# Rounding weights on ScalarE, loading them through Pool's queue, and new rules for VectorE's pieces

## The chip, the core and the metric

One core of one Trainium2 chip. The metric is the device time of one execution in microseconds (us); for the kernel before it is 1285.2 us, the median of three runs (1283.07 to 1286.11). Engines: TensorE (PE; PEld is its weight load), VectorE (DVE), ScalarE (ACT), GpSimd (POOL, "Pool"), SyncE (SP). SP computes nothing here and issues most of the DMAs, in order. Every engine works through its own instructions in order; between engines there are semaphores.

## The reference

`x` is 2048 x 512. The output is `g * a + (1 - g) * b`, where `g` is a sigmoid per row, `a` is attention and `b` a two-layer network on the same `x`:

```
g = sigmoid((x * gate_w).sum(-1))
q = (x @ wq) as 32 heads of 16;  k = x @ wk;  v = x @ wv        # one k and v for all heads
a = softmax(q k^T / 4) v, heads side by side, @ wo              # 32 x 2048 x 2048 exponentials
h = relu(x @ w1 + b1)^2                                          # 512 -> 1792
b = h @ w2 + b2                                                  # 1792 -> 512
```

All in float32.

## The kernel before

**Precision.** A float32 matrix `w` is split in two tiles: `r`, rounded to the multiplier's format, and `l = w - r`. A product is three matmuls, `r r + r l + l r` (`pairs`, L174). `split` (L170) does both steps on VectorE: L171 rounds, L172 subtracts.

**Attention.** Work is cut in 32 iterations `it`: chunk `c` of 512 query rows (4) by group of 4 heads (8). Each has 32 units `u`, half a chunk of queries against 128 keys. `scores` (L598) runs two matmuls into a bank pair `s` (two such pairs exist), and ScalarE takes the exponential of 128 x 1024 (L609). `context` (L612) multiplies the exponentials into `acc` (L620). `finish` (L637) copies `acc` with ScalarE (L647, for each iteration but the last two), and `unpack` (L220) separates outputs `oc` from denominators `lc` with two DMAs on SP. `divide` (L628) divides on VectorE, in `pieces` of 128 columns, four for a pair of iterations; then Pool's queue stores the result `oTs` (L662). `ask` (L700) loads it back and splits it, and `projection` (L731) multiplies by `wo`.

**The network.** `hidden` (L508) computes one tile of `h` (128 of the 1792 columns) for one chunk from one w1 tile; `summed` (L531) adds a group of four or three tiles into the chunk's result with their w2 tiles. Over the four chunks, 56 w1 tiles and 56 w2 tiles of 128 x 512 are loaded and split (n counts them). `w_load` (L414) allocates one float32 tile per half, `w1f` or `w2f`, and loads it on SP's queue; `w_split` (L421) rounds and subtracts on VectorE and asks for the next load, so a tile's load begins when its predecessor has been split. `room` says how many split tiles may exist.

**The order.** The program is written out by a planner at build time. `stream` (L181) turns the network, the q products and the projections into slots: one slot is two matmuls of 64 rows, half 0 now and half 1 five slots later (`LAG`). A unit has 12 slots in general, 9 where `summed` has three tiles. When a half is complete, its evacuation is issued to VectorE at once. There are three PSUM banks for units, of which each takes two. `phase` (L795) puts together some units of attention and some slots: a full phase has 4 score units and 8 slots, a light phase 2 units and 2 or 3 slots. `plan` (L817) chooses by the slots that are left: the first 174 phases are full, the others light. At the head of each phase stand a piece of division from `side` and then `turn_of_chores` (L493): first what is in `soon`; then `w_split` for tiles whose load is due by the planner's own clock (`w_ready`: more than `LANDS` = 4 us since issue; a phase counts 4.9 or 2.1 us); then one of the `chores` (loading and splitting `x` again for chunks 2 and 3, `wo`, and attention results). A chore that loads holds up the others for 6 us of that clock. If the generator reaches a tile that isn't split, `have` (L489) splits it on the spot.

If `projection` must wait for `ask`, it yields None and the phase's remaining slots are empty.

The loads of q for the next iteration (L406), `unpack`, the weight loads, and the loads of `x`, `wo` and `oT` share SP's queue. Pool's queue has stores, and the scaling of `b2` (L541, four per chunk).

At most two things of this kind were given out at the head of a full phase, one in a light one (`count`, L497).

Of the kernel before, what the change touches and what calls it, by code (L numbers as in the profile page):

```python
# [23 lines left out]
NG = 8  # L24
# [9 lines left out]
WARM = 12  # L34
LANDS = 4.0
# [5 lines left out]
Q_ROWS = (0, 0, DH), (DH, 0, DH), (RS + 1, DH + 1, KS), (RS, DH, DH + 1)  # L41

# [100 lines left out]
def mix_kernel(ctx: ExitStack, tc: tile.TileContext, xT, wkv, wq, wo, w12, b1, b2, cst, out):  # L143
# [16 lines left out]
    ok = keep.tile([128, NC * KT * 4], F32, name="ok")  # L160
# [85 lines left out]
    with fast, tc.tile_pool(name="at", bufs=1) as at, \  # L246
# [163 lines left out]
        wf, since, ws = ({}, {}), ({}, {}), ({}, {})  # L410
# [3 lines left out]
        def w_load(half):  # L414
            n = len(wf[half])
            if n < NC * NF:
                wf[half][n] = at.tile([128, 512], F32, name=f"w{half + 1}f")
                since[half][n] = clock
                nc.sync.dma_start(wf[half][n], w12[n % NF, :, half * 512:half * 512 + 512])

        def w_split(half):  # L421
            n = len(ws[half])
            assert n < room[half]
            ws[half][n] = [at.tile([128, 512], F32R, name=f"w{half + 1}{x}", bufs=3 + half) for x in "rl"]
            split(*ws[half][n], wf[half][n])
            w_load(half)

        def w_ready(half):
            n = len(ws[half])
            return n in since[half] and n < min(room[half], NC * NF) and clock - since[half][n] > LANDS  # L430

# [50 lines left out]
        held = 0.0  # L482
        chores, soon = [], [lambda: wq_split(2, nc.vector), lambda: wq_split(3, nc.vector), lambda: w_load(0), lambda: w_load(1)]
# [9 lines left out]
        def turn_of_chores(slots):  # L493
# [3 lines left out]
            count = 2 if slots > 3 and (not side or w_ready(0) and w_ready(1)) else 1  # L497
            if soon:
                return soon.pop(0)()
            for half in (1, 0):  # L500
                if count and w_ready(half):
                    w_split(half)
                    count -= 1
            if count and chores and clock > held:
                if chores.pop(0)():
                    held = clock + LANDS + 2

        def hidden(c, f, hs):  # L508
# [5 lines left out]
            (wr, wl), (r, l) = ws[0][n], x[c]  # L514

# [40 lines left out]
        def x_again(c):  # L556

            r, l = [xp.tile(sh, F32R, name=f"x{n}again{c}", tag=f"x{n}{c - 2}") for n in "rl"]
            f = []

            def load():
                f.append(keep.tile(sh, F32, name="xf", tag="r2"))
                nc.sync.dma_start(f[0], xT[:, c * CH:(c + 1) * CH].rearrange("(k p) s -> p k s", p=128))
                return True

            def part(k):
                split(r[:, k], l[:, k], f[0][:, k])
# [3 lines left out]
            chores.append(load)  # L571
            for k in range(KT):
                later(part, k)
# [50 lines left out]
        ol = {}  # L624
# [284 lines left out]
```

## Time and profile before

| | |
|---|---|
| median of the runs | 1285.2 us (1283.07 to 1286.11) |
| the profiled execution's own time | 1283.75 us |
| its span, first to last instruction | 1281.7 us |
| mean granted TensorE clock | 0.986 |
| busy: TensorE / ScalarE / VectorE / Pool | 1250.9 / 1014.0 / 630.2 / 59.9 us |
| DMA moved | 85.58 MB, 67 GB/s mean |

How to read the lines of the profile below. A group: line, engine, operation, written tile <- read tiles, shape, x count, then | busy us, mean ns of one | idle time just before them, and what ended it. A wait: who waited, <- for whom: us in total, times, longest. A row of a timeline: start, duration, engine, line, operation, x count, and in brackets idle time before it and what ended that. SPq means SP's instruction queue. A window: start:end, length, then the busy time (and count) of each engine in the order PE, PEld, DVE, ACT, POOL, then granted clock, DMA share and GB/s; a window of one source line shows only the engine that has it. A row of the chain of waits: start, duration, what it was. DMA rows: tile, engine, count, KB each, median us from issue to landing.

### The profile page before, as it was taken

Reading aid. Unit: us, or ns where it says so; the run is one execution under the profiler, and the core shown is the slowest. Engines: PE = TensorE matmul, PEld = TensorE weight load, DVE = VectorE, ACT = ScalarE, POOL = GpSimd, SP = SyncE. Lnnn points to the kernel's source line nnn. Section 1 sums busy time; section 2 is a strip of 40 time slices with the busy share of each in tenths; the row PEclk is TensorE's granted clock in tenths of the full one; section 3 lists DMA queues with packets and bytes.
Section 4 is the critical chain, followed back from the end, with each engine's and each line's share of the span. In section 5 each row is a group of like instructions: output and inputs, shape, how many; then the busy total and the mean of one; then the engine's idle time right before and its main releaser. Section 6 shows DMA issues by size and latency. Waiting matters only on the chain.

```text
span 1281.7 us, 23432 instructions
## 1 busy us (share of the span) xinstructions
PE 1250.9 (98%) x9702; PEld 622.2 (49%) x9702; DVE 630.2 (49%) x1173; ACT 1014.0 (79%) x1083; POOL 59.9 (5%) x68
## 2 busy tenths in 40 slices
PE   7999999999999999999999999999999999999997
PEld 5555545554555555445555555555433333333333
DVE  6454664727567544466745576256262344231412
ACT  5678778786777777767877777877899999999984
POOL 1001120000002000000010000002000000000000
PEclk9799999998999999999999999999999999999998
DMA  6243321202122121112212122122010120010100
GB/s 203 78 127 86 97 96 38 87 24 73 63 104 82 47 88 47 44 57 92 87 54 71 46 91 71 55 77 73 29 61 29 38 87 30 30 54 30 54 34 35
DMA packets 46563, 85.58 MB, mean 67 GB/s; under 512 B 11828, under 2 KB 13492, under 8 KB 45940
## 3 DMA queue, kind: packets, MB, share of 16 engines
q1 hardware_dynamic: 39348, 68.28, 16.4%
q0 software_dynamic: 6816, 15.23, 3.5%
q8 instruction: 78, 1.28, 0.4%
q10 hardware_dynamic: 288, 0.52, 0.1%
q14 instruction: 33, 0.27, 0.1%
HBM read 55.15 MB, written 20.97 MB: 59 GB/s over the span
## 4 chain that ended last, share of the span: by engine, by line
PE 89%; DVE 5%; DMA 2%; SPq 1%; issue 1%; ACT 0%; DVEq 0%; ACTq 0%
PE acc L620 35%; PE mm L207 29%; PE s L605 23%; DMA w2f<-in_w 1%; PE mm L179 1%; SPq L406 1%; DVE n L634 1%; DVE w2l L172 1%; DMA wof<-in_wo 1%; DMA xf<-in_xT 0%; DVE w2r L171 0%; DVE big L521 0%; DVE w1l L172 0%; DVE big L522 0%; DVE hr L172 0%
## 5 line engine op out<-in xcount | busy, mean ns | idle before, releaser
L609 ACT ACTIVATE e<-s 128x1024 f32<-128x1024 f32 x1024 | 981.0, 1023 | 226.4 <-PE s L605 222.7
L620 PE MATMUL acc<-e,v_ext 128*32 128x512 f32 x4096 | 510.8, 602 | 0.0
L605 PE MATMUL s<-qa,k_aug 49*128 49x512 f32 x2048 | 460.9, 438 | 5.0 <-DMA qa<-qs 4.8
L605 PEld LDWEIGHTS s<-qa,k_aug 49*128 49x128 f32 x2048 | 198.6, 186 | 344.2 <-ACT e L609 313.9
L544 DVE SCALAR_TENSOR_TENSOR res<-mm,omg,res 128x512 f32<-128x512 f32 x128 | 96.0, 750 | 269.0 <-PE mm L207 269.0
L207 PE MATMUL mm<-w2r,hr 64*128 64x512 f32 x896 | 214.3, 396 | 4.8 <-DVE big L517 3.9
L620 PEld LDWEIGHTS acc<-e,v_ext 128*32 128x32 f32 x4096 | 98.7, 109 | 207.3 <-issue 203.6
L207 PE MATMUL mm<-w2l,hr 64*128 64x512 f32 x448 | 160.1, 395 | 0.0
L207 PEld LDWEIGHTS mm<-w2r,hr 64*128 64x128 f32 x896 | 130.3, 188 | 22.2 <-DVE big L517 4.8
L207 PEld LDWEIGHTS mm<-w2l,hr 64*128 64x128 f32 x448 | 84.2, 188 | 7.3
L207 PE MATMUL mm<-xr,w1r 64*128 64x512 f32 x224 | 77.5, 394 | 4.4 <-DVE big L521 2.4
L207 PE MATMUL mm<-xragain,w1l 64*128 64x512 f32 x224 | 79.5, 391 | 0.0
L207 PE MATMUL mm<-xragain,w1r 64*128 64x512 f32 x224 | 78.5, 393 | 0.9 <-DVE big L517 0.8
L207 PE MATMUL mm<-xlagain,w1r 64*128 64x512 f32 x224 | 78.7, 391 | 0.0
L207 PE MATMUL mm<-xr,w1l 64*128 64x512 f32 x224 | 78.5, 391 | 0.0
L207 PE MATMUL mm<-xl,w1r 64*128 64x512 f32 x224 | 78.0, 392 | 0.0
L521 DVE TENSOR_TENSOR big<-big,mm 128x512 f32<-128x512 f32 x56 | 38.4, 686 | 79.8 <-PE mm L207 79.7
L517 DVE TENSOR_SCALAR big<-mm,b1t 128x512 f32<-128x512 f32 x56 | 42.0, 750 | 49.9 <-PE mm L207 47.9
L634 DVE RECIPROCAL n<-n 128x128 f32<-128x128 f32 x60 | 57.2, 953 | 2.1
L171 DVE CAST w2r<-w2f 128x512 fp32r<-128x512 f32 x56 | 23.6, 421 | 51.4 <-DMA w2f<-in_w 51.3
L207 PEld LDWEIGHTS mm<-xr,w1r 64*128 64x128 f32 x224 | 41.3, 186 | 10.7 <-DVE big L521 3.4
L207 PE MATMUL mm<-xr,wqr 64*128 64x512 f32 x120 | 44.4, 424 | 1.9 <-DVE qf L369 1.9
(137 smaller groups left out, 1128.6 us busy)
## 6 DMA issues: line engine op xcount, KB each, us to landing
w1f<-in_w SPq DMA_DIRECT2D x56, 256.0 KB
w2f<-in_w SPq DMA_DIRECT2D x56, 256.0 KB
qa<-qs SPq DMA_DIRECT2D x192, 64.0 KB
xf<-in_xT SPq DMA_DIRECT2D x8, 512.0 KB
qs<-qr SPq DMA_DIRECT2D x16, 256.0 KB
ress<-res POOLq DMA_DIRECT2D x4, 1024.0 KB, 4.2
qs<-ql POOLq DMA_DIRECT2D x15, 256.0 KB, 8.6
oc<-accs SPq DMA_DIRECT2D x30, 128.0 KB
```

Of the source, the lines that this page charges most:

```text
L171: nc.vector.tensor_copy(r, src)
L172: nc.vector.tensor_tensor(l, src, r.bitcast(F32), OP.subtract)
L179: nc.tensor.matmul(ps, a, b, start=first and i == 0, stop=last and i == len(terms) - 1)
L207: nc.tensor.matmul(banks[half], a[rows], b[rows], start=i == 0, stop=i == len(terms) - 1)
L406: nc.sync.dma_start(q[64 * r + row:64 * r + row + b - a].bitcast(F32), qs[it, r, a:b])
L517: nc.vector.tensor_scalar(h[0], p, b1t[:, f:f + 1], None, op0=OP.add)
L521: nc.vector.tensor_tensor(h[0], h[0], p, OP.add)
L544: nc.vector.scalar_tensor_tensor(part, p, omg[:, s:s + 1], part, op0=OP.mult, op1=OP.add)
L605: nc.tensor.matmul(s[:, r].rearrange("p (a n) -> p a n", a=2), k_aug[rows, kt * 128:(kt + 1) * 128], qa[it][rows, :, cols], start=True, st ...
L609: nc.scalar.activation(es[u // 2][:, :, cols], s.rearrange("p r (a n) -> p (r a) n", a=2), AF.Exp, scale=SCALE)
L620: nc.tensor.matmul(acc[h * 32:(h + 1) * 32, cols], v_ext[:, i % NK], es[i][:, h % 2 * 2 + h // 2, cols], start=(i % NK == 0), stop=(i % NK ...
L634: nc.vector.reciprocal(n, n)
```

## The change

- Each half (w1, w2) now has two float32 places and loads two tiles ahead: `w_load` of tile n+2 goes to the place of tile n, right behind n's subtraction. The second place of each half lies in a new tile `stage`, which takes the buffer (tag `r2`) that held whole loads of `x`, `wo` and `oT`. These now come in halves of two tiles, through the other half of `stage`.
- The weight loads are issued on Pool's queue (`nc.gpsimd`) and no longer on SP's.
- The split is parted: `w_round` rounds, `w_rest` subtracts on VectorE and issues the load. In full phases the rounding is an ACTIVATE Copy on ScalarE, issued at the end of the phase, behind its last exponential, for each half that is ready; the subtraction follows at the head of the next phase. In light phases, and where `have` forces a tile, both stay on VectorE.
- `turn_of_chores` counts a budget of VectorE time per phase (2.7, or 2.4 in light phases; 1.2 less with a division at hand; 0.7 per subtraction, 1.1 per split). A chore needs more than 1.0 left. Which half goes first depends on how many w1 tiles are ahead.
- A division comes in six parts of 86 columns (the last of 82), and the generator idles one turn before the first in full phases, two in light ones. The store is issued with the last part, no longer one turn behind it.

```diff
+BUDGET = 2.7
+PARTS = [slice(a, min(a + 86, CH)) for a in range(0, CH, 86)]
...
         def w_load(half):
             n = len(wf[half])
             if n < NC * NF:
-                wf[half][n] = at.tile([128, 512], F32, name=f"w{half + 1}f")
+                if n < 2:
+                    if n and not stage:
+                        stage.append(keep.tile(sh, F32, name="stage", tag="r2"))
+                    place = stage[0][:, 2 + half] if n else at.tile([128, 512], F32, name=f"w{half + 1}f")
+                else:
+                    place = wf[half][n - 2]
+                wf[half][n] = place
                 since[half][n] = clock
-                nc.sync.dma_start(wf[half][n], w12[n % NF, :, half * 512:half * 512 + 512])
+                nc.gpsimd.dma_start(wf[half][n], w12[n % NF, :, half * 512:half * 512 + 512])
+
+        def w_round(half, copy):
+            n = len(rounded[half])
+            assert n < room[half]
+            rounded[half][n] = [at.tile([128, 512], F32R, name=f"w{half + 1}{x}", bufs=3 + half) for x in "rl"]
+            copy(rounded[half][n][0], wf[half][n])
+
+        def w_rest(half):
+            n = len(ws[half])
+            r, l = ws[half][n] = rounded[half][n]
+            nc.vector.tensor_tensor(l, wf[half][n], r.bitcast(F32), OP.subtract)
+            w_load(half)
+
+        def scalar_copy(out, src):
+            nc.scalar.activation(out, src, AF.Copy)
 
         def w_split(half):
...
+            if len(rounded[half]) == len(ws[half]):
+                w_round(half, nc.vector.tensor_copy)
+            w_rest(half)
...
-            count = 2 if slots > 3 and (not side or w_ready(0) and w_ready(1)) else 1
             if soon:
                 return soon.pop(0)()
-            for half in (1, 0):
-                if count and w_ready(half):
+            spare = (BUDGET if slots > 3 else BUDGET - 0.3) - (1.2 if side else 0.0)
+            for half in halves():
+                if len(rounded[half]) > len(ws[half]):
+                    w_rest(half)
+                    spare -= 0.7
+                elif slots < 4 and spare > 1.0 and w_ready(half):
                     w_split(half)
-                    count -= 1
-            if count and chores and clock > held:
+                    spare -= 1.1
+            if spare > 1.0 and chores and clock > held:
                 if chores.pop(0)():
                     held = clock + LANDS + 2
+
+        def halves():
+            return (0, 1) if len(ws[0]) < begun[0] + 2 else (1, 0)
...
         def x_again(c):
...
+            def load(a):
+                nc.sync.dma_start(stage[0][:, :2], xT[a * 256:a * 256 + 256, c * CH:(c + 1) * CH]
+                                  .rearrange("(k p) s -> p k s", p=128))
                 return True
...
         def pieces(it, c, t, o, l):
-            for _ in range(2):
+            for _ in range(1 if many[0] else 2):
                 yield
-            for q in range(4):
-                i = 4 * (4 * c + t) + q
-                divide(t, o, l, slice(q * 128, q * 128 + 128), ok[:, i:i + 1])
-                yield
+            for q, cols in enumerate(PARTS):
+                i = len(PARTS) * (4 * c + t) + q
+                divide(t, o, l, cols, ok[:, i:i + 1])
+                if q < len(PARTS) - 1:
+                    yield
             nc.gpsimd.dma_start(oTs[it - 1:it + 1].rearrange("u d n -> (u d) n"), o)
...
             for u in us:
                 scores(u)
+            for half in halves():
+                if slots > 3 and not soon and w_ready(half):
+                    w_round(half, scalar_copy)
```

More of the change, by code (lines that the diff above doesn't have):

```diff
@@ L159, in mix_kernel @@
     b1t = keep.tile([128, NF], F32, name="b1t")
-    ok = keep.tile([128, NC * KT * 4], F32, name="ok")
+    ok = keep.tile([128, NC * KT * len(PARTS)], F32, name="ok")
     bad = keep.tile([1, 1], I32, name="bad")
@@ L407, in q_load @@
             qa[it] = q
-        wf, since, ws = ({}, {}), ({}, {}), ({}, {})
+        wf, since, rounded, ws = ({}, {}), ({}, {}), ({}, {}), ({}, {})
+        stage = []
         room = [3, 4]
@@ L514, in hidden @@
             (wr, wl), (r, l) = ws[0][n], x[c]
+            begun[0] += 1
             def first(p):
@@ L622, in context @@
                                      skip_group_check=True, tile_position=(0, h * 32))
-        ol = {}
+        ol, many = {}, [True]
         complete = set()
@@ L628, in divide @@
         def divide(t, o, l, cols, okc):
-            n = at.tile([128, 128], F32, name="n")
+            n = at.tile([128, 86], F32, name="n")[:, :cols.stop - cols.start]
             nc.vector.tensor_scalar(n, l[:, cols], L_MIN, L_MAX, op0=OP.max, op1=OP.min)
@@ L706, in ask, with load @@
             tiles = []
-            def load():
-                tiles.extend((keep.tile(sh, F32, name="oT", tag="r2"), keep.tile(sh, F32R, name="orr", tag="r3"),
-                              xp.tile(sh, F32R, name="orl", tag="xl3")))
-                nc.sync.dma_start(tiles[0][:, :n], oTs[c * NG:c * NG + 2 * n].rearrange("(t u) d n -> (u d) t n", u=2))
+            def load(a):
+                if a == 0:
+                    tiles.extend((keep.tile(sh, F32R, name="orr", tag="r3"), xp.tile(sh, F32R, name="orl", tag="xl3")))
+                m = min(2, n - 2 * a)
+                i = c * NG + 4 * a
+                nc.sync.dma_start(stage[0][:, :m], oTs[i:i + 2 * m].rearrange("(t u) d n -> (u d) t n", u=2))
                 return True
             def part(t):
-                oT, orr, orl = tiles
-                split(orr[:, t], orl[:, t], oT[:, t])
+                orr, orl = tiles
+                split(orr[:, t], orl[:, t], stage[0][:, t % 2])
                 if t == n - 1:
                     osp[c] = orr, orl
-            chores.append(load)
             for t in range(n):
+                if t % 2 == 0:
+                    chores.append(lambda t=t: load(t // 2))
                 later(part, t)
@@ L798, in phase @@
             us = list(us)
+            many[0] = slots > 3
             if ripe:
```

41 lines of the change are left out of this document (17 added, 24 removed).

## The prediction

> **What bounds the kernel now.** First the busy times of the page:
>
> ```profile
> PE 1250.9 (98%) x9702; PEld 622.2 (49%) x9702; DVE 630.2 (49%) x1173; ACT 1014.0 (79%) x1083; POOL 59.9 (5%) x68
> ```
>
> TensorE is busy 98% of the span, so a change that only moves elementwise work can win no more than what TensorE loses in holes, in stretches at a lower granted clock, and at the ends. Those losses I measured in phases. A full phase holds four exponentials, so the count of exponentials in a stretch, divided by four, gives its phases. These windows begin and end at the first context matmul of a phase, taken from the chain of waits; up to one exponential straddles an edge. The columns are us, ACT busy (count), granted clock, DMA share, GB/s:
>
> ```profile
> 44.95:910.01 865.06, 654.75 (x688) 0.99 0.22 72
> 817.30:910.08 92.78, 72.24 (x77) 1.00 0.17 58
> 49.91:78.37 28.46, 19.44 (x21) 0.94 0.41 126
> 161.87:189.36 27.49, 19.17 (x21) 1.00 0.31 103
> 282.18:318.63 36.45, 23.23 (x25) 0.91 0.23 77
> 524.62:561.46 36.84, 23.26 (x25) 0.95 0.23 76
> 688.73:704.69 15.96, 11.49 (x13) 1.00 0.33 109
> ```
>
> The quiet stretch (second row) has 19 phases in 92.78 us: 4.883 us each. All the full phases (first row) are 172 in 865.06 us; at 4.883 they would take 839.9. So 25.1 us are lost, and the five stretches below hold nearly all: 28.46 - 5 x 4.883 = 4.0; 27.49 - 5 x 4.883 = 3.1; 36.45 - 6 x 4.883 = 7.2; 36.84 - 6 x 4.883 = 7.5; 15.96 - 3 x 4.883 = 1.3. Together 23.1. The rest, 2.0, lies scattered in pieces of 0.2 to 0.5 us.
>
> What ends last there? Next, the largest DMA and queue pieces of the chain of waits, each inside one of the five stretches (and one context row, the edge at which the third begins):
>
> ```profile
> 57.29 8.49 DMA w2f<-in_w
> 172.71 7.51 DMA wof<-in_wo
> 282.18 1.86 PE acc L620 x16
> 289.78 2.58 DMA w2f<-in_w
> 531.03 1.33 SPq L406
> 533.10 2.55 DMA w2f<-in_w
> 696.70 2.44 DMA w2f<-in_w
> ```
>
> All five are late loads of weights. The timelines of SP and VectorE for the third stretch say how:
>
> ```profile
> 285.94 3.40 SPq L406 DMA_DIRECT2D qa<-qs  x8
> 289.78 10.32 SPq L419 DMA_DIRECT2D w2f<-in_w  x3
> 285.67 0.75 DVE L517 TENSOR_SCALAR big<-mm,b1t 128x512 f32<-128x512 f32 x1 [2.85 <-PE mm L207]
> 292.38 0.43 DVE L171 CAST w2r<-w2f 128x512 fp32r<-128x512 f32 x1 [5.96 <-DMA w2f<-in_w]
> 305.00:310.00 5.00, 3.04 (x18) 1.98 (x14) 4.83 (x12) 1.38 (x2) 0.00 (x0) 0.79 0.28 105
> ```
>
> The load of w2f is queued on SP behind the q loads, and is issued only at 289.78. It takes 2.6 us. VectorE, which issues in order, stands 5.96 us at the rounding of that tile, with the evacuations of TensorE's banks behind it. It then works off the backlog (4.83 of 5 us busy in 305 to 310), TensorE runs dry (3.04 of 5), and the granted clock falls to 0.79. Over the run there are 14 such waits, and SP's own waits show what its loads stand behind, above all the unpacking that waits for ScalarE's copy of the context:
>
> ```profile
> DVE w2r L171 <- DMA w2f<-in_w: 51.3, 14, 6.8
> SPq L222 <- ACT accs L647: 354.5, 30, 29.1
> ```
>
> **The change, part by part.** *Loads two tiles ahead, on Pool's queue.* A tile's successor is now loaded while the tile between them is still unused, and SP's waits no longer hold it back. Pool has stores of the same 256 KB in two forms, listed with KB and median us to landing:
>
> ```profile
> oTs<-oc POOLq DMA_DIRECT2D x15, 256.0 KB, 2.3
> qs<-ql POOLq DMA_DIRECT2D x15, 256.0 KB, 8.6
> L662 POOL DMA_DIRECT2D oTs<-oc x15: 539/542/625, 150.6 to 1208.7; - x15
> DMA to landing us min/median/max: 6.9/8.6/11.5
> ```
>
> (The last row is that of the q stores.) A weight tile is 128 rows of 2 KB without the q stores' scatter, so I take 2.3, and keep 6.9 to 11.5 as the other bound. Is it in time? Count from a phase's first scores. The tightest case is the third and fourth w2 tile of a group, rounded one per phase. ScalarE's copies of the phase before end by 0.56 (below), two subtractions of 0.69 end by 1.9, the load lands at 1.9 + 2.3 = 4.2, and its copy is due behind the exponentials of the next phase, at 2 x 4.88 - 0.48 = 9.3. Slack 5.1 us. So I let the five losses go, but for an allowance of 0.5 us: -22.6. Bounds: 0 (the lateness only moves) to -25.1.
>
> What else moves past Pool: its stores and the four scalings L541 now share a queue with loads that wait for a subtraction. Each such wait is for VectorE work emitted earlier than the evacuations that need Pool's results, so I cost it at 0; if that cover goes, an evacuation of a group's first unit waits up to 1.7 us, at four places.
>
> *Rounding on ScalarE.* The rows are the group of the exponentials, ScalarE's timeline, then groups for a copy in SBUF, the cast that it replaces and the subtraction that stays, and two rows of TensorE's timeline:
>
> ```profile
> L609 ACT ACTIVATE e<-s 128x1024 f32<-128x1024 f32 x1024 | 981.0, 1023 | 226.4 <-PE s L605 222.7 <-PE mm L207 3.2 <-ACT e L609 0.2
> 399.51 3.80 ACT L609 ACTIVATE e<-s 128x1024 f32<-128x1024 f32 x4 [1.08 <-PE s L605]
> 404.41 3.78 ACT L609 ACTIVATE e<-s 128x1024 f32<-128x1024 f32 x4 [1.10 <-PE s L605]
> 408.82 0.60 ACT L647 ACTIVATE accs<-acc 128x512 f32<-128x512 f32 x1 [0.63 <-PE acc L620]
> 409.32 2.85 ACT L609 ACTIVATE e<-s 128x1024 f32<-128x1024 f32 x3
> L434 ACT ACTIVATE wqr<-wqf 128x512 fp32r<-128x512 f32 x4 | 2.5, 616 | 0.0
> L171 DVE CAST w2r<-w2f 128x512 fp32r<-128x512 f32 x56 | 23.6, 421 | 51.4 <-DMA w2f<-in_w 51.3
> L172 DVE TENSOR_TENSOR w2l<-w2f,w2r 128x512 fp32r<-128x512 f32 x56 | 38.8, 692 | 1.9
> 403.79 0.50 PE L605 MATMUL s<-qa,k_aug 49*128 49x512 f32 x2
> 401.50 0.19 PEld L605 LDWEIGHTS s<-qa,k_aug 49*128 49x128 f32 x2 [0.20 <-ACT e L609]
> ```
>
> ScalarE idles 1.08 to 1.10 us ahead of each phase's first exponential, waiting for its scores; the copies are put exactly there. Four exponentials of 1.02 take 3.79, so neighbours overlap by 0.10. One copy adds 0.52, two add 1.04: both fit. (The exponentials of one phase end at 403.31, the next phase's scores begin at 403.79 and its first exponential at 404.41: 0.48 before and 0.62 after the scores; two copies thus end 0.56 after them.) The last score of a phase already waits 0.20 us for an exponential (last row), so any overrun would lengthen the phase one for one. How many double phases? A w1 and a w2 tile are each used once in 24 slots, three phases. The 174 full phases (a count of the planner's own numbers: slots left fall by 8, units by 4) have 1392 slots, less 180 for q and 96 for two projections: 46 tiles and some four ahead, so about 50 copies of each kind. The w2 copies come four in a row, w1 every 1.5 phases: some 33 doubles. Fully serial copies (2 x 0.616) would overrun by about 0.16: at most 5.3 us; with overlap 0. Where `accs` falls as well (21 phases, only 0.63 free ahead of it), a single copy fits, a double is late by about 0.41: 21 x 33/174 = 4 times, 1.7, at most 2.4. I take +2.0, bounds 0 to 7.7. The about 100 casts that leave VectorE (100 x 0.42 = 42 us) are worth nothing by themselves, because in quiet phases TensorE does not wait for VectorE.
>
> *The subtraction now waits for the copy.* Before, VectorE ran ahead and split weights before a phase began; now up to two subtractions stand at the phase's start until ScalarE is through, to 1.9 us into it, and behind them are evacuations. With units of 12 slots, a first half ends at slot 4 or 8 and its bank is wanted five slots on, in the next phase: 3 us of slack. Units of 9 slots (groups of three) can end at slot 1 to 3 and want the bank back within the same phase: an evacuation of 0.75 behind 1.9 misses by up to 0.6. Some 24 such units lie in full phases, half of them badly placed, not all with two subtractions: +1.0, bounds 0 to 4.
>
> *Division in six, pieces counted per phase, loads in halves.* Six pieces of 86 columns are the same work in smaller bites. With the first idle turn dropped in full phases the store comes at the same turn (2 + 4 + 1 before, 1 + 6 now); in light phases it comes one later (2 + 6). The halved loads through `stage` add a wait of three light phases to the last chunk. The halves of `x_again` and of `wo` come two or three full phases later too, but `x_again` has a whole chunk (42 phases) until it is read, and `wo` is first read in the next chunk: 0; without that cover, 4.9 us a phase. In the last chunk the chain is exposed:
>
> ```profile
> 1208.75 0.54 POOL L662 DMA_DIRECT2D oTs<-oc  x1 [46.52 <-DVE oc L635]
> 1211.06 0.40 SPq L711 DMA_DIRECT2D oT<-oTs  x1
> 1217.62 3.83 ACT L609 ACTIVATE e<-s 128x1024 f32<-128x1024 f32 x4 [0.19 <-PE s L605]
> 922.36:1116.29 193.93, 176.43 (x183) 1.00 0.15 49
> ```
>
> A light phase takes 193.93 / 91.5 = 2.12 us with two slots and about 1.9 without (four exponentials in 3.83 + 0.19). Before, slots already ran out around 1217 while the last attention output was fetched. Four more phases (one of the division, three of the second load) lose eight slots: each phase gains 0.24, the eight slots are done later at about 0.23 us: +1.9 - 1.0 = +0.9, bounds 0 to 1.9.
>
> *A rule against the change.* The Trainium skill (SBUF — State Buffer, section "SBUF: two separate sides") warns that a DMA issued from the GpSimd queue has its descriptors written by GpSimd, which a VectorE copy in two-port mode locks out; the page's example goes from about 620 to about 3100 ns. The trace here does not show it, with 0.54 to 0.63 us per issue. By the rule, an estimate from that page, a load would land 2.5 us later, still inside the slack, and the sum would stand; were several such blocks to add up, the first rival below would come nearer.
>
> **The sum**, against the profiled execution's own time: 1283.75 - 22.6 + 2.0 + 1.0 + 0.9 = 1265.05. The median of the runs is 1.45 above the profiled one (1285.2), so I forecast 1266.5.
>
> **The rivals.** *Pool's loads land late, and ScalarE stalls (slower).* Place: the copies of the third and fourth w2 tile, about 26 times. The following exponential is due at 2 x 4.88 + 0.62 = 10.4, and the copy must start 0.52 before it; so it bites from a landing of about 8 us on and decides from 8.7. At 8.6 a stall is 0.6 (16 us in all: 1282, still just faster), at 10 it is 2.0 (52 us: 1318), at 11.5 it is 3.5 (91 us: 1357). For it: the q stores' landing. Against: the plain stores' 2.3 and the loose 5.1. Chance 0.08 for the slower outcome.
>
> *Half the stalls stay.* VectorE was busy 4.83 of 5 us late in the third stretch, with divisions, two splits and evacuations. If its own load matters as much as the wait, or the copies overrun at their upper bound, some 11 us of the 22.6 remain: 1277.8. For it: that saturation. Against: it comes right after the wait, and a phase now has at most two subtractions (1.4) where it had two splits (2 x 1.11 = 2.2). Chance 0.17.
>
> *The change does not do what it says:* the tiles are still not there and the wait moves unchanged from VectorE to ScalarE. Nothing is won: 1285 if nothing is paid either, 1289 with the 3.9 of costs. For it: the first tiles are still loaded during the crowded start. Against: a load is now due two tiles ahead. 0.06.
>
> *Better:* all 25.1 go and nothing is paid: 1260.1; 0.05.
>
> **How the numbers follow.** Forecast 0.64 (1261 to 1272), half 0.17, late loads 0.08, no effect 0.06, better 0.05. Between versions of this kernel 0.2%, 2.6 us, is about what a measurement can tell from nothing. Faster: 0.64 + 0.17 + 0.05 = 0.86. The no-effect case splits, 0.05 same and 0.01 slower; slower with the late loads 0.09. The range, 1260 to 1278, takes in the best case and half the stalls, and leaves out the rest.
>
> **What would show it.** Right: the windows around the five stretches show 4.88 us per phase and clock 1.0; the wait of `w2r` for its DMA is gone from VectorE and has not come up on ScalarE; ScalarE's idle ahead of the first exponential falls by about 0.5 per copy; Pool's weight loads land in about 2.3 us. Wrong: `ACT w2r <- DMA w2f` among the waits (first rival); TensorE waiting for evacuations `L544` or `L517` in phases with two subtractions (second rival); quiet phases longer than 4.9 us (copies not hidden); more than four slotless phases near the end.

## The result and the profile after

The changed kernel takes 1264.76 us (median of 4 runs, 1264.25 to 1264.97), against 1285.5 us for the kernel before (4 runs, 1283.07 to 1286.11). The ratio is 0.9845, with a 95% interval of 0.983 to 0.986: some 20 us or 1.55% faster. The profiled execution took 1264.82 us with a span of 1262.98; before it was 1283.75 and 1281.72. The prediction's sum, which was made against the profiled execution, ended at 1265.05. The forecast of 1266.5 lies 1.7 above the measured median: it added 1.45 because the median of the kernel before lay above its profiled execution, and in the changed kernel the two agree to 0.06.

The same sections of the span can be laid beside each other. "Start" goes to the first context matmul, "full phases" are the next 172 phases, "excess" is their time above 172 x 4.883 = 839.9 (the length of a quiet phase), "light phases" go to the last context matmul, "end" is the rest. All in us:

| section | before | after | difference |
|---|---|---|---|
| start | 44.95 | 45.37 | +0.42 |
| full phases | 865.06 | 844.74 | -20.32 |
| of which excess | 25.19 | 4.87 | -20.32 |
| light phases | 354.87 | 354.86 | -0.01 |
| end | 16.84 | 18.01 | +1.17 |
| span | 1281.72 | 1262.98 | -18.74 |

First the busy times on the page of the kernel after:

```profile
PE 1240.3 (98%) x9702; PEld 616.8 (49%) x9702; DVE 610.8 (48%) x1227; ACT 1062.6 (84%) x1179; POOL 119.2 (9%) x180
```

ScalarE has 96 instructions more, the 96 copies of full phases, and 48.6 us more work. VectorE has 19.4 us less work in 54 instructions more: it lost the casts and gained short division instructions. TensorE has the same instructions and is done sooner.

Next, the windows of the kernel after over all its full phases (first row) and over the phases that correspond to the five stretches of the prediction. The columns are us, ScalarE's busy time on exponentials (count), granted clock, DMA share, GB/s:

```profile
45.37:890.12 844.75, 653.99 (x688) 1.00 0.24 74
50.44:75.20 24.76, 19.06 (x21) 1.00 0.44 128
163.81:188.21 24.40, 19.04 (x21) 1.00 0.35 101
276.13:305.97 29.84, 22.87 (x25) 1.00 0.26 77
512.32:541.95 29.63, 22.88 (x25) 1.00 0.27 78
669.40:684.92 15.52, 11.50 (x13) 1.00 0.44 116
```

With 5, 5, 6, 6 and 3 phases of 4.883 taken off, 0.3, 0.0, 0.5, 0.3 and 0.9 remain: 2.1 where it was 23.1. The granted clock, which had been 0.91 to 0.95 in three of them, is 1.00 in all five.

The waits of the kernel after show what became of the late loads, and what has grown instead (us in total, times, longest us):

```profile
ACT e L639 <- PE s L635: 160.9, 284, 4.9
DVE w2l L440 <- ACT w2r L444: 40.6, 24, 2.5
DVE n L661 <- DMA lc<-accs: 29.4, 15, 3.5
DVE w1l L440 <- ACT w1r L444: 17.6, 27, 1.4
DVE w2r L435 <- DMA w2f<-in_w: 4.2, 2, 2.1
```

VectorE's waits for the load of a w2 tile were 51.3 us in 14 times, up to 6.8; two remain, 4.2 in all. For ScalarE's copies the list of waits has no row for a load. ScalarE's idle time before its exponentials has gone from 222.7 to 160.9: that is what the copies filled. VectorE has a new wait, 58.2 us in 51 times, for ScalarE's copy; and its wait for the load ahead of a division's first piece is up from 10.6 us (5 times) to 29.4 (15 times).

The timeline of ScalarE in the third stretch shows the copies in place (start, us, engine, line, operation; idle before in brackets):

```profile
287.20 0.63 ACT L444 ACTIVATE w1r<-w1f 128x512 fp32r<-128x512 f32 x1
287.71 0.63 ACT L444 ACTIVATE w2r<-w2f 128x512 fp32r<-128x512 f32 x1
288.38 3.82 ACT L639 ACTIVATE e<-s 128x1024 f32<-128x1024 f32 x4
292.08 0.63 ACT L444 ACTIVATE w1r<-stage 128x512 fp32r<-128x512 f32 x1
292.60 0.63 ACT L444 ACTIVATE w2r<-stage 128x512 fp32r<-128x512 f32 x1
293.26 3.80 ACT L639 ACTIVATE e<-s 128x1024 f32<-128x1024 f32 x4
298.14 1.94 ACT L639 ACTIVATE e<-s 128x1024 f32<-128x1024 f32 x2 [1.08 <-PE s L635]
```

Two copies fit between two phases, with the exponentials still 4.88 us apart (288.38, 293.26, 298.14); the last row is a phase without copies and its idle 1.08.

The loads on Pool's queue land in about 3 us (the page's list of DMA issues; KB each, median us from issue to landing; the last row is for the line of these loads, L429):

```profile
stage<-in_w POOLq DMA_DIRECT2D x56, 256.0 KB, 2.9
w2f<-in_w POOLq DMA_DIRECT2D x28, 256.0 KB, 3.3
DMA to landing us min/median/max: 2.6/2.9/9.4
```

The slowest, 9.4 us, was issued at 57.7 us, in the crowded start. That is beyond the 8 us at which the prediction let a stall begin for its tightest tile, and the first stretch still lost only 0.3.

### The profile page after: what moved, and what is told of

It reads as the page before. It is cut to its first block, busy times and chain, and to the rows that moved or that the text cites. A ratio compares the mean times of both kernels' runs of the same rounds, so it can differ in the third digit from the quotient of the medians.

```text
span 1263.0 us, 23769 instructions
## 1 busy us (share of the span) xinstructions
PE 1240.3 (98%) x9702; PEld 616.8 (49%) x9702; DVE 610.8 (48%) x1227; ACT 1062.6 (84%) x1179; POOL 119.2 (9%) x180
## 3 DMA queue, kind: packets, MB, share of 16 engines
q0 software_dynamic: 15776, 44.60, 10.8%
## 4 chain that ended last, share of the span: by engine, by line
PE 92%; DVE 4%; ACT 2%; DMA 1%; issue 0%; SPq 0%; DVEq 0%; ACTq 0%
PE acc L650 37%; PE mm L210 30%; PE s L635 24%; ACT e L639 2%; PE mm L182 1%; DMA lc<-accs 1%; DMA xf<-in_xT 1%; DVE n L664 0%; DVE w1l L440 0%; DVE w2l L440 0%; PE s L321 0%; DVE big L552 0%; DVE k_aug L315 0%; PE s L182 0%; DVE big L548 0%
## 5 line engine op out<-in xcount | busy, mean ns | idle before, releaser
L639 ACT ACTIVATE e<-s 128x1024 f32<-128x1024 f32 x1024 | 980.2, 1023 | 162.3 <-PE s L635 160.9
L635 PE MATMUL s<-qa,k_aug 49*128 49x512 f32 x2048 | 455.7, 436 | 5.8 <-DMA qa<-qs 4.1
L635 PEld LDWEIGHTS s<-qa,k_aug 49*128 49x128 f32 x2048 | 196.0, 185 | 345.0 <-ACT e L639 314.3
L552 DVE TENSOR_TENSOR big<-big,mm 128x512 f32<-128x512 f32 x56 | 38.4, 686 | 77.5 <-PE mm L210 77.3
L664 DVE RECIPROCAL n<-n 128x86 f32<-128x86 f32 x90 | 61.9, 688 | 3.1
L429 POOL DMA_DIRECT2D stage<-in_w x56 | 30.7, 548 | 191.8 <-DVE w1l L440 126.8
L210 PEld LDWEIGHTS mm<-xr,w1l 64*128 64x128 f32 x224 | 41.7, 186 | 4.4
```

The lines of the kernel that those rows point to most:

```text
L210: nc.tensor.matmul(banks[half], a[rows], b[rows], start=i == 0, stop=i == len(terms) - 1)
L429: nc.gpsimd.dma_start(wf[half][n], w12[n % NF, :, half * 512:half * 512 + 512])
L552: nc.vector.tensor_tensor(h[0], h[0], p, OP.add)
L635: nc.tensor.matmul(s[:, r].rearrange("p (a n) -> p a n", a=2), k_aug[rows, kt * 128:(kt + 1) * 128], qa[it][rows, :, cols], start=True, st ...
L639: nc.scalar.activation(es[u // 2][:, :, cols], s.rearrange("p r (a n) -> p (r a) n", a=2), AF.Exp, scale=SCALE)
L664: nc.vector.reciprocal(n, n)
```

## The experiments

The change bundles five things: Pool's queue, the second tile of lead, rounding on ScalarE, the new count of VectorE's pieces, and the division in six with one idle turn less. The theory of the prediction (theory 1) is that the late loads cost the time and that their removal is the gain; 1a says that the second tile of lead removes them, 1b that the queue does. Its rival (theory 2) is that VectorE's own load mattered as much, so that moving the casts is the gain. Theories 3 to 5 came up on the way and are told in the expectations. Each kernel was timed beside the kernel before on the same chip; ratios are against that kernel, with their 95% intervals. "Excess" is that of the full phases, as above.

### Rounding on VectorE again

```diff
-                    w_round(half, scalar_copy)
+                    w_round(half, nc.vector.tensor_copy)
```

> The kernel after, with the rounding at a full phase's end given back to VectorE (about 96 casts of 0.42 us, 40 us of VectorE; ScalarE loses 61 us). Theory 1 (late loads were the whole loss; VectorE's own work was never the limit): 1264 to 1267 us, the two phases with a context copy and two roundings lose their 0.32 us each, a few more evacuations come late. Theory 2 (VectorE's own load was half of it): back to 1272 to 1278, with VectorE over 4.7 us busy in 5 and TensorE waiting for L548 or L552 around 290 to 310 and 540 to 560.

Measured: 1264.28 us, ratio 0.9848 [0.9832, 0.9865]; the kernel after has 0.9845. The window over the full phases of this kernel:

```profile
45.67:889.97 844.30, 653.24 (x688) 1.00 0.24 74
```

The excess is 4.4 against 4.9. With the rest of the change in place, moving the rounding to ScalarE neither brings nor costs anything that can be measured. The rival theory, as far as the casts go, falls.

### The lead alone, on SyncE's queue

```diff
-                nc.gpsimd.dma_start(wf[half][n], w12[...])
+                nc.sync.dma_start(wf[half][n], w12[...])
```

> The kernel after, with the weight loads issued on SP's queue again, still two tiles ahead. Theory 1a (two tiles ahead is enough on its own: 4.5 us of slack against SP's 3.4 us of q loads): 1265 to 1269. Theory 1b (the queue is the cause, being ahead does not help a load that is not issued): 1274 to 1285, and ScalarE waits for a weight load.

Measured: 1263.67 us, ratio 0.9844 [0.9827, 0.986], a little below what was expected. The window over its full phases:

```profile
45.17:889.35 844.18, 653.79 (x689) 1.00 0.24 74
```

The excess is 4.3. With two tiles of lead the queue does not matter: SyncE still waits for ScalarE's copy of the context (330.4 us in 30 times, against 354.5 before), and so holds the loads behind it back, but by less than the lead. VectorE's waits for `w2f` are 3.3 us in two times.

### The queue alone, one tile ahead

```diff
-                    place = stage[0][:, 2 + half] if n else at.tile([128, 512], F32, name=f"w{half + 1}f")
+                    place = wf[half][0] if n else at.tile([128, 512], F32, name=f"w{half + 1}f")
                 else:
-                    place = wf[half][n - 2]
+                    place = wf[half][n - 1]
...
-        chores, soon = [], [..., lambda: w_load(0), lambda: w_load(1), lambda: w_load(0), lambda: w_load(1)]
+        chores, soon = [], [..., lambda: w_load(0), lambda: w_load(1)]
```

> The kernel after, with one place per half: a tile's load is issued when its predecessor has been subtracted, still on Pool's queue. A half can then be rounded only every other phase, so four w2 tiles take eight phases where five and a half are there, and the last are forced on VectorE. Theory 1a (being ahead is the gain): 1275 to 1285, VectorE or ScalarE waits for loads. Theory 1b (the queue is the gain): 1265 to 1270.

Measured: 1264.70 us, ratio 0.9847 [0.9831, 0.9863]. The window over its full phases:

```profile
45.64:890.72 845.08, 653.93 (x688) 1.00 0.25 73
```

The excess is 5.2. Theory 1a is refuted as a necessary condition: Pool's queue with one tile of lead does the same. Each of the two halves of the edit is enough by itself, beside the rest of the change. VectorE still waits for `w2f` here, 15.3 us in five times and at most 3.9; a short wait need not lengthen a phase.

### Only the queue, in the kernel before

```diff
-                nc.sync.dma_start(wf[half][n], w12[...])
+                nc.gpsimd.dma_start(wf[half][n], w12[...])
```

> The kernel before, with one word changed: the weight loads on Pool's queue. In the stalls at 282 to 318 and 524 to 561 the load would then be issued right behind its predecessor's subtraction (282.8), land about 2.9 later (285.8), and VectorE would be there at 286.4: no wait. The stalls at 50 to 78 (a load that took 8.5 us in the crowded start) and at 162 to 189 would stay. Theory 1b (queue): 1283.75 - 7.2 - 7.5 - 1.3 = 1268, so 1266 to 1271. Theory 1a (being ahead is needed): 1278 to 1286. Theory 2 (VectorE's own load): 1274 or more, with VectorE saturated without any wait for a load.

Measured: 1269.35 us, ratio 0.9892 [0.9876, 0.9909], as 1b has it. Windows of this kernel over all full phases, the start and the third stretch:

```profile
43.96:894.19 850.23, 653.96 (x689) 1.00 0.25 73
48.83:77.06 28.23, 19.42 (x21) 1.00 0.43 127
278.34:309.80 31.46, 23.43 (x25) 1.00 0.26 73
```

One word of code recovers some 15 of the 20 us (14.7 against the kernel before on the same chip). The excess is 10.3. Of it, 3.8 stay in the first stretch (28.23 - 5 x 4.883), where the start is crowded, and 2.2 in each of the two places where a chunk's divisions meet the splits (31.46 - 6 x 4.883; the fourth stretch is as long); before they had been 7.2 and 7.5. So the size of the two large stalls was set by the wait for the load, and a smaller part by the work around it.

### Neither the queue nor the lead

The diffs of the second and third experiment together, on the kernel after.

> The kernel after with both changes to the loads undone: SP's queue and one place per half. Rounding, budget and divisions stay as in the kernel after. Theory 3 (either change to the loads makes them timely enough, and one of the two is needed): the lateness returns, now on ScalarE as well, 1274 to 1286, with waits for w2f of 4 us and more. Theory 4 (the loads are not what is needed once VectorE's pieces are counted and a half is rounded only every other phase): 1264 to 1267.

Measured: 1272.85 us, ratio 0.9917 [0.99, 0.9935]; neither theory has it. Windows of this kernel over all full phases and over the third stretch, then its waits for loads of `w2f`:

```profile
43.90:897.52 853.62, 654.32 (x689) 1.00 0.24 73
281.98:311.29 29.31, 22.79 (x25) 1.00 0.25 76
```

```profile
DVE w2r L435 <- DMA w2f<-in_w: 23.1, 6, 6.9
ACT w2r L444 <- DMA w2f<-in_w: 4.8, 2, 4.4
```

The excess is 13.7. The large stalls of the third and fourth stretch have not come back (29.31 - 6 x 4.883 = 0.0) though the loads have the old queue and the old lead. What comes back is in the start, where two phases between 88 and 104 us are long by 4.5 and 1.8, and ScalarE waits 4.4 us for a tile; three places more are long by about 1 us, and the rest is scattered. So something else in the changed kernel also protects those two places. This may be a third property: a phase's end rounds a tile, and the subtraction that frees its place, and so issues the next load, comes with VectorE's pieces of the next phase; a load then has one and a half to two phases before its tile is rounded. Before, it had one: `w_ready` lets a tile be split from 4.0 us of the planner's clock after its load is issued, which is one phase of 4.9, while on SyncE 3.40 us of q loads stood ahead of the load and its landing took 2.58 (the prediction's rows): 6.0. That is theory 5. This run does not part it from the new count and the division in six, which the kernel has too; the next one tests it alone.

The whole distance was longer than 6.0. These rows of the kernel before are the subtraction that allowed the load, and SyncE's first instruction after it:

```profile
282.13 0.69 DVE L172 TENSOR_TENSOR w2l<-w2f,w2r 128x512 fp32r<-128x512 f32 x1
284.73 0.47 SPq L222 DMA_DIRECT2D oc<-accs  x1
```

The load could have been issued at 282.82. SyncE then still waited for the context's copy, issued the two unpacking DMAs and the q loads, and VectorE could round the tile at 292.38, 9.6 us later, having waited 5.96. One phase of 4.9 is too little for that. In the kernel of this section the same tile is rounded 9.0 us after that point, in the next one 12.0, and neither waits for it.

### One number in the kernel before

```diff
-            return n in since[half] and n < min(room[half], NC * NF) and clock - since[half][n] > LANDS
+            return n in since[half] and n < min(room[half], NC * NF) and clock - since[half][n] > 8.0
```

> The kernel before with one number changed: a weight tile counts as landed 8 us after its issue by the planner's clock, not 4, so it is split two phases after its load was asked for, not one. Loads stay on SP's queue, one tile ahead. Theory 5 (what was wrong was the time between a load's issue and its use: one phase of 4.9 us, against 3.4 us of q loads ahead of it on SP and 2.6 to land; any edit that gives it two phases removes the stalls): the two stalls of 7.2 and 7.5 us go and the start's shrinks, 1266 to 1272. Rival: four w2 tiles at one per two phases do not fit between two sums, the last are split on the spot and wait for their load: 1278 to 1290.

Measured: 1268.32 us, ratio 0.9877 [0.986, 0.9894], as theory 5 has it. The window over all full phases and the wait that was 51.3 us in 14 times:

```profile
45.41:894.56 849.15, 653.59 (x689) 1.00 0.24 73
```

```profile
DVE w2r L171 <- DMA w2f<-in_w: 10.3, 4, 6.0
```

The excess is 9.3. No load is issued earlier and no queue is changed; the tile is only asked for one phase later, and 16 us of the 20 are won. The two large stalls were a matter of the planner's distance between a load and its use; what stays at those places is 2.1 each, much as with only the queue changed (2.2).

### The old count of VectorE's pieces

The loads, the lead and the six parts of the kernel after, with the old rule: one piece a turn or two, each a whole split on VectorE, nothing at a phase's end.

```diff
-            spare = (BUDGET if slots > 3 else BUDGET - 0.3) - (1.2 if side else 0.0)
-            for half in halves():
-                if len(rounded[half]) > len(ws[half]):
-                    w_rest(half)
...
+            count = 2 if slots > 3 and (not side or w_ready(0) and w_ready(1)) else 1
+            for half in (1, 0):
+                if count and w_ready(half):
                     w_split(half)
...
-            for half in halves():
-                if slots > 3 and not soon and w_ready(half):
-                    w_round(half, scalar_copy)
```

> The kernel after with its loads and its six-part divisions, but the old rule at the head of a phase (a count of one or two whole splits on VectorE, no rounding at a phase's end). It has the loads of the kernel after and VectorE's load of the kernel before. Theory 3: the late loads are gone, what returns is VectorE's crowding next to divisions, 2.1 us at each of two places as in the kernel before with Pool's queue, less what it loses now (0.5): 1265 to 1269. Theory 4: most of the gain is the new rule's, 1272 to 1282.

Measured: 1266.32 us, ratio 0.9862 [0.9846, 0.9879], as expected. The excess is 6.4 against 4.9: two phases, at 302 and 538 us, are long by 1.5 each. The new count, with the rounding at a phase's end, is worth about 1.5 us.

### Two idle turns before a division again

```diff
-            for _ in range(1 if many[0] else 2):
+            for _ in range(2):
```

> The kernel after with two idle turns ahead of a division in full phases too, as in the kernel before. In the kernel after VectorE waited 15 times, 29.4 us in all, for the lc DMA ahead of a division, and phases near 438 and 684 us are 0.32 and 0.57 us long where a TensorE bank waits for VectorE behind it. If the earlier turn causes this, the waits fall to about 5 and 10 us and the two excesses go: 1263.5 to 1264.5. If not, waits and excess stay.

Measured: 1263.28 us, ratio 0.984 [0.982, 0.9859]. The window over its full phases, and the wait ahead of a division:

```profile
45.70:888.79 843.09, 654.33 (x689) 1.00 0.24 74
```

```profile
DVE n L661 <- DMA lc<-accs: 10.8, 5, 3.5
```

The wait falls from 29.4 us in 15 times to 10.8 in 5, as before the change (10.6 in 5), and the excess from 4.9 to 3.2. Dropping the turn had made the first piece of a division start before its data was there; VectorE stood, and evacuations behind it came late. The time by itself would not show it, since the interval overlaps that of the kernel after. One of two long phases that were expected to become normal did (0.57 us at 684); the other, 0.32 at 438, stayed: there the context's copy and two weight copies fall together on ScalarE.

### Four parts

```diff
-PARTS = [slice(a, min(a + 86, CH)) for a in range(0, CH, 86)]
+PARTS = [slice(a, a + 128) for a in range(0, CH, 128)]
```

> The kernel after with a division in four parts of 128 columns again (1.8 us each on VectorE and not 1.3), the rest as after. The parts were expected to be worth nothing by themselves: 1264 to 1266. If the smaller bites are what keeps evacuations in time beside two subtractions, the phases around 290 to 310 and 535 to 545 us lengthen by 1 to 2 us each: 1267 to 1270.

Measured: 1267.71 us, ratio 0.9871 [0.9856, 0.9886]. Three microseconds are lost; three phases, at 302, 539 and 688 us, are long by 1.8, 1.9 and 1.4, the places where divisions and splits meet. The small pieces are worth about 3 us by the medians (the excess is 9.0 against 4.9). This holds with the one idle turn of the kernel after: VectorE waits 3.40 us for a division's data at 282.7 us, as it does there, and has no gap of more than 0.11 us from then until past 300. What the pieces are worth with two idle turns no run shows.

### Every rounding on ScalarE twice

Each copy is issued a second time, with the same result.

```diff
-            nc.scalar.activation(out, src, AF.Copy)
+            for _ in range(2):
+                nc.scalar.activation(out, src, AF.Copy)
```

> The kernel after with every rounding on ScalarE done twice (0.52 us more each, the result is the same). ScalarE has 1.10 us of idle time ahead of a phase's first exponential. If that is the whole of the slack and an overrun lengthens the phase one for one: 47 phases with one rounding stay free (1.04), 19 with two overrun by 2.08 - 1.10 = 0.98, 7 with a context copy and one by about 0.4, 2 with a context copy and two by 1.0 more: +19 + 3 + 2 = +24, 1287 to 1291. If ScalarE were already on the path, all 96 would show: +50. If there were more slack than the idle time shows: under +10.

Measured: 1289.16 us, ratio 1.0041 [1.0026, 1.0056]. ScalarE's timeline in this kernel:

```profile
289.08 3.77 ACT L640 ACTIVATE e<-s 128x1024 f32<-128x1024 f32 x4
292.73 1.30 ACT L445 ACTIVATE w1r<-w1f 128x512 fp32r<-128x512 f32 x2
293.93 1.28 ACT L445 ACTIVATE w2r<-w2f 128x512 fp32r<-128x512 f32 x2
295.12 3.75 ACT L640 ACTIVATE e<-s 128x1024 f32<-128x1024 f32 x4
```

A phase with four copies is 295.12 - 289.08 = 6.04 us long, 1.16 more than 4.883. There are 19 such phases (18 are long by 1.13 to 1.15 and one by 1.48, 21.9 in all); phases with two copies, 25 of `w1r` alone and 22 of `w2r` alone, lose nothing. Where the context's copy falls as well, one weight tile (two copies) costs 0.44, seven times, and two tiles 1.63, twice. The idle time of 1.1 us a phase is a real slack with a sharp edge: two copies cost nothing, four cost all that lies beyond it.

### Loads that land late

Each load goes from memory to memory and then on chip, both on Pool's queue; the additional copy in memory is the only change. Pool, which works in order, issues the second step only when the first has landed.

```diff
+    bounce = [dram.tile([128, 512], F32, name=f"bounce{h}") for h in range(2)]
...
-                nc.gpsimd.dma_start(wf[half][n], w12[...])
+                nc.gpsimd.dma_start(bounce[half], w12[...])
+                nc.gpsimd.dma_start(wf[half][n], bounce[half])
```

> The kernel after with each weight load made in two steps on Pool's queue, DRAM to DRAM and then to its place, so that it lands about 3 to 4 us later. By the slack worked out for the tightest tile (5.1 us at a landing of 2.3, so 4.5 at the 2.9 measured) a single load stays in time: 1264 to 1268. By the rival of late loads a copy on ScalarE stalls from a landing of 8 us on: where both halves load in one phase the second of them lands after 2 x 3.5 + 2.9 us and is late by about 2: at most 15 such cases, so up to 1295, with ScalarE waiting for in_w in the waits.

Measured: 1298.04 us (2 runs), ratio 1.011 [1.009, 1.0131], beyond both expectations. Windows of this kernel over its full phases and over a part of the start, then its waits:

```profile
44.11:921.68 877.57, 655.14 (x689) 0.99 0.34 101
68.68:135.43 66.75, 31.02 (x33) 0.85 0.45 122
```

```profile
PE s L637 <- ACT e L641: 18.2, 7, 6.3
ACT w2r L446 <- DMA stage<-bounce: 13.9, 2, 8.9
ACT w2r L446 <- DMA w2f<-bounce: 9.0, 1, 9.0
```

Of 37.7 us of excess, 27.7 lie in the second window (66.75 - 8 x 4.883). Three copies on ScalarE wait 9.0, 8.9 and 5.0 us for their tile, and TensorE's scores wait behind ScalarE. This is the mechanism of the first rival. In the quiet rest of the run, with twice the loads on the queue, the excess is 37.7 - 27.7 = 10.0, where the kernel after has 4.9 in all: 5 us or so.

### What is best of both

SyncE's queue, two idle turns (one for the last pair), no second weight copy in a phase that has the context's copy, and the three tiles of the last chunk in one load.

```diff
+                nc.sync.dma_start(wf[half][n], w12[...])
...
+            for _ in range(2 if it < NC * NG - 3 else 1):
...
+                m = min(2, n - 2 * a) if c < NC - 1 else n
...
+                    if ending[0]:
+                        break
```

> The kernel after with four small edits that the runs so far point to: weight loads on SP's queue, two idle turns ahead of a division as before (one for the last pair), no second rounding in a phase that also has a context copy, and the last chunk's three attention tiles loaded at once. If the effects add (about -1.0 and -1.0 as single runs had it, -0.6 for the two long phases, -0.9 for three slotless phases at the end): 1261 to 1262.5. If SP's queue and the idle turn won nothing but noise: 1263 to 1264.5.

Measured: 1261.69 us (5 runs, 1260.6 to 1262.8), ratio 0.9825 [0.9812, 0.9838]: the fastest kernel here, some 3 us below the changed one and within what was expected if the effects add. The window over its full phases:

```profile
45.17:888.74 843.57, 653.71 (x688) 1.00 0.24 74
```

Of the gain in its span, 2.4 us, 1.2 lie in the full phases (843.57 against 844.75) and 1.06 at the end; light phases are unchanged (354.85 against 354.86), so loading the last three tiles at once brought nothing there. Of the 1.06 at the end, 0.57 came with SyncE's queue alone (second experiment); the other 0.49 need not be the edits', because the last 6 us of computing had a granted clock of 0.70 here and of 0.54 there.

## Why the prediction was right, and where its steps were not

**The losses of late loads, -22.6.** Place and cause were right. In the five stretches 21.0 of 23.1 went (2.1 stay), so the allowance of 0.5 was 1.6 too small. The step's reason was only half right: it gave the lead and Pool's queue together as what puts the loads in time. The runs show that either alone does (second and third experiment), and that without both the rest of the change still keeps the two large stalls away and about half of the gain (1272.85). One phase more between a load and its use, alone, wins 16 us (`w_ready` in the kernel before, with 8.0 for 4.0). The common cause is that in the kernel before a load had one phase, 4.9 us, for what took 9.6 in the third stretch.

**Landing.** I took 2.3 us from Pool's plain stores; the loads take 2.9 to 3.3 in the median. The slack of 5.1 covered the difference.

The Trainium skill (SBUF — State Buffer, section "SBUF: two separate sides") warns that a VectorE copy in two-port mode keeps GpSimd from writing the descriptors of its DMAs; the prediction's estimate from that page was 2.5 us more for a load. Nothing of that size is seen: the 112 issues on Pool take 536 to 763 ns in the kernel after. With only the queue changed, where all the casts stay on VectorE, they take 536 to 699 ns and the loads land in 3.0 to 3.2 us in the median. Whether these casts run in two-port mode the profile does not tell.

**Rounding on ScalarE, +2.0.** Sized too high. The slack that it rests on was right, as the doubled copies show. The count of phases with two copies was wrong: 33 and four with the context's copy were predicted, 19 and 2 came, since the two kinds of tiles fall together less often than assumed. In the kernel after the 19 are long by 0.33 in all and the two by 0.32 each: about 1.0. That the casts' leaving VectorE is worth nothing by itself was right (first experiment).

**The subtraction behind the copy, +1.0.** Six phases, at 301, 350, 449, 537, 586 and 685 us, are long by 0.34 to 0.57, together 2.6, each with a wait of TensorE's weight loads for a late evacuation. The timeline of VectorE and of the weight loads at 297 to 300 us of the kernel after shows one:

```profile
296.27 0.68 DVE L440 TENSOR_TENSOR w2l<-stage,w2r 128x512 fp32r<-128x512 f32 x1
296.87 0.74 DVE L548 TENSOR_SCALAR big<-mm,b1t 128x512 f32<-128x512 f32 x1
297.53 0.26 DVE L661 TENSOR_SCALAR n<-lc 128x86 f32<-128x86 f32 x1
...
298.84 0.25 DVE L665 TENSOR_TENSOR oc<-oc,n 128x86 f32<-128x86 f32 x1
299.01 0.68 DVE L552 TENSOR_TENSOR big<-big,mm 128x512 f32<-128x512 f32 x1
```

```profile
299.74 0.18 PEld L210 LDWEIGHTS mm<-w2r,hr 64*128 64x128 f32 x1 [0.73 <-DVE big L552]
```

VectorE has no gap from the subtraction to the evacuation L552; a piece of a division stands between them, and TensorE waits 0.73. Where VectorE lost the time shows earlier in the kernel after (first row), and the same evacuation is on time in the kernel with two idle turns, where VectorE waits for TensorE (second row):

```profile
283.73 0.21 DVE L661 TENSOR_SCALAR n<-lc 128x86 f32<-128x86 f32 x1 [3.28 <-DMA lc<-accs]
298.80 0.69 DVE L552 TENSOR_TENSOR big<-big,mm 128x512 f32<-128x512 f32 x1 [1.23 <-PE mm L210]
```

After the 3.28 us spent on the division's data VectorE has no gap of more than 0.11 us until TensorE's wait. The mechanism, a late evacuation behind the subtractions, was right, but the step named the wrong thing ahead of it: in this phase the subtractions do not wait for ScalarE's copy at all. About 1.7 of the excess disappears with the idle turn given back (4.87 to 3.21; four of the six phases become normal), so much of this term belongs to the next one.

**Division in six, 0.** This was the step that failed: "the same work in smaller bites". The bites are worth 3 us (four parts: +3), because evacuations stand behind a shorter piece where a chunk's divisions and the weight pieces meet; the dropped idle turn costs about 1.5, because the division's data is then late (29.4 us of waits). The two meet at the same places, and how they add was not tried. The prediction's removal of the losses in the five stretches rests in part on the first: with four parts the five stretches keep 6.2 (0.4, 0.0, 2.2, 2.0 and 1.7), not 2.1. The new count of VectorE's pieces, which had no term, is worth another 1.5 (the kernel with the old count). Differences of 1.5 are below what the timing tells, since the intervals overlap, and 3 is at the edge; it is the long phases and the waits in the traces, at the places named, that support them.

**The end, +0.9.** The end is 1.17 longer, but not by slotless light phases: light phases take 354.86 against 354.87. The price comes from Pool, as the last section shows. Right in size, wrong in cause.

**How the sum came out.** Measured on the profiled executions, 1264.82 - 1283.75 = -18.93, predicted -18.70. The difference is made of: late loads +1.6 (-21.0 for -22.6); the rest of the full phases -2.3 (its excess went from 2.1 to 2.8, +0.7, where +3.0 was predicted for the copies and the evacuations); the start +0.4, which had no term; the end +0.3; what lies around the span -0.2. Errors of 1.6 and 2.3 with opposite signs cancel, and the agreement to 0.2 is luck; that to 2 or 3 is not.

**The rivals.** Late loads on Pool: the mechanism exists, but its place is the crowded start and not the third and fourth tile of a group, and it needs about twice the landing time or more (the kernel with two steps for each load). Half the stalls stay: the saturation of VectorE is there, but it is worth 1.5 to 3 us (old count, four parts), or 4.3 when both are as before (the 2.2 at two places with only the queue changed), not 11. The change does nothing: refuted by the windows.

What stays open is how much of the planner's distance (the tile asked for a phase later), of the lead and of the queue protects each place in the start; one of them at a time was tried only in whole kernels.

## What to carry to other kernels

Where an in-order engine waits for a load, work out from the trace the distance from the moment at which the load may be issued to its landing, with all that stands ahead of it on its queue, and compare it with the distance that the planner leaves: here 9.6 us against 4.9, and one constant recovered 16 of 20 us. Idle time ahead of a phase on another engine was free up to its length here and cost one for one beyond, so count how often two pieces meet there. An idle turn or a size of a piece that looks like the same work has a price where several deadlines meet, and it is best tried alone.

## What the runs showed of the hardware

I had not expected the loads on Pool's queue to lengthen the end of the program. Near the end, while the last outputs are being computed, Pool starts a long drain; these are the rows of the kernel before, of the kernel after, and of the kernel after with the loads on SyncE (duration in ns min/median/max, first and last start in us):

```profile
L905 POOLq DRAIN  x3: 40/107/3830, 1273.5 to 1281.5; - x3
```

```profile
L942 POOLq DRAIN  x3: 40/107/7587, 1254.6 to 1262.7; - x3
```

```profile
L942 POOLq DRAIN  x3: 40/107/3830, 1252.8 to 1261.3; - x3
```

It takes 3.83 us without the weight loads on Pool and 7.59 with 112 of them. Every kernel here with the loads on SyncE has 3.83, every one with them on Pool 7.59, and the one with two DMAs for each load 8.08. In the kernel after it starts at 1254.6 and ends at 1254.6 + 7.59 = 1262.2; in each kernel with these loads on Pool it ends 0.8 us before the span does. With SyncE's queue it ends at 1252.8 + 3.83 = 1256.6, when the last outputs are just being issued, and the span runs on to 1261.6. The part of the drain that the last outputs do not cover makes the end longer: 16.84 to 17.44 us with SyncE and 17.96 to 18.42 with Pool (18.87 with twice the DMAs), 1.12 between the kernel before and the same with only the queue changed, 0.57 between the kernel after and the same with SyncE's queue. What the drain does in that time the profile does not show.
